# Attention, expert and gated feed-forward in one kernel: the rare-case branch moved to the end, one subtraction moved later in its step, the window limits loaded in one transfer, and other filler matmuls

## The chip, the cores and the metric

The kernel runs on one core of a Trainium2 chip. The metric is the device time of one execution in microseconds; the time before is 661.46 us, the median of three runs (661.29 to 661.57). TensorE's clock has two levels, 1.2 and 2.4 GHz; profiles give it as a granted share, 0.50 or 1.00.

## The reference

Three layers follow each other, in float32.

```python
# 1. attention: 2 batches x 8 heads, 768 positions, head size 64
keep = is_sink | in_window          # the first n_sink=4 keys, or the last window=128
scores = np.where(keep, scale * q @ k.T, -1e9)
x = softmax(scores) @ v             # -> 1536 tokens x 512
# 2. one expert out of 8 per token (argmax of cosine logits), w1 512x1024, w2 1024x512
out[mask] = gate_w[mask, None] * (np.maximum(x[mask] @ w1[e], 0.0) @ w2[e])
# 3. gated feed-forward, 512 -> 1536 -> 512
return ((x @ w_a) * (x @ w_b)) @ w_out
```

n_sink and window are inputs (64-bit integers). The weights of layer 3 arrive as 64-bit floats.

## The kernel before, in words

All products that carry weights run as three matmuls on split operands (high x high, high x low, low x high), so each operand is rounded to a high part and the rest is kept as a low part. After `tc.manual_schedule()` each engine executes its instructions in the order in which the Python code issues them, so this order is the schedule.

**Start.** SP issues the first loads: halves of the first q and k tiles, and between them two broadcasts of n_sink and window (8 bytes to each of 128 partitions each, L193 and L194) into `ctli`. VectorE turns these into float limits and masks (`early_masks`, L222 to L229); the first softmax step (L474) needs the mask. Meanwhile `warm_pe` (L964) issues filler transposes of the identity on TensorE: 8, 4 and 3 of them ahead of the first scores (`WARM`), then 6, 3, 4 and 1 in the first four attention steps (`WARMG`).

**Attention.** 12 blocks of 128 queries with 4 steps each; a step computes two heads' scores (L465; L459 in block 0), softmax, transposes (L490), and the product with v (L521). The block's normalisation and routing (L539 and others) follow some steps later.

**Experts.** Tokens are sorted into slots by expert; the number of slots per expert is planned for common cases. A list `seq` sets the order of matmul groups, and a generator `side_gen` computes the tables for the last layer between them: where each token's row lies in DRAM (`cidx`, and `cide` clipped for the first four tiles), where the output row goes (`ctok`), the squared gate (`gsq`) and a flag `cnt`, which is above zero if limits or expert loads are outside the plan.

**Branch.** After the experts every engine loads `cnt` (L1473) and meets `tc.If(ns_v > 0)` (L1475). Its body recomputes what the plan did not cover and stores rows again; it is not entered with these inputs, so every engine jumps over it.

**Feed-forward.** Three groups of 512 tokens, and for each 12 slices f of 128 hidden units: `ab_mms(f)` makes the two 128x512 products a and b (24 matmuls, L1600 to L1602), `g_split` multiplies them and splits the result, `out_mms` adds the slice to four output tiles (12 matmuls, L1620 to L1622) one slice later. TensorE's order is ab(0), ab(1), out(0), ab(2), out(1) and so on. In the first group `conv_step` also converts the weights of slice f+2 from 64-bit floats, in two half steps per slice; each is a rounding to the high part on ScalarE (`wh`, L1399), two bit operations for the next half (`conv_b0`, L1384 and L1385), the low part (`wl`, L1401) and two further bit operations (`conv_b1`, L1390 and L1391) on VectorE. `g_split` of slice f stands between the two half steps:

```python
nc.scalar.copy(asb, ab[0])
nc.vector.tensor_tensor(out=asb, in0=ab[1], in1=asb, op=ALU.mult)    # L1609
nc.scalar.copy(gh, asb)                                             # L1612
EL[el].tensor_tensor(out=gl, in0=asb, in1=gh, op=ALU.subtract)      # L1613, VectorE
```

The output rows leave by GpSimd's indirect DMAs (L1667).

Of the kernel before, what the change touches and what calls it, by code (L numbers as in the profile page):

```python
# [10 lines left out]
F32 = mybir.dt.float32  # L11
# [51 lines left out]
WARM = [8, 4, 3]  # L63
WARMG = [6, 3, 4, 1]
# [38 lines left out]
TINY = 2.0 ** -15 * 1.125  # L103

# [19 lines left out]
def tile_kernel(ctx, tc, q, k, v, n_sink, window, emb, tau, w1, w2, wc, out, dbg=None):  # L124
# [62 lines left out]
    tt = pc.tile([E, 1], F32, name="tt")  # L187
    q0, k0 = new_q(0, 0), new_k(0, 0)
    for a in (0, W2):
        ld(q0, q, 0, 0, a, a + W2)  # L190
        ld(k0, k, 0, 0, a, a + W2)
        if a == 0:
            nc.sync.dma_start(ctli[:, 0:2], n_sink.bitcast(I32).partition_broadcast(P))  # L193
            nc.sync.dma_start(ctli[:, 2:4], window.bitcast(I32).partition_broadcast(P))  # L194
# [767 lines left out]
    def warm_pe(n):  # L962
        for _ in range(n):
            nc.tensor.transpose(wps, ident, ident)  # L964
# [206 lines left out]
    fe = pool(ctx, "fe", side="right")  # L1171

    def side_gen(w_, pl, psp, tag):
# [172 lines left out]
        V.tensor_copy(cide, cpos[:, 0:4])  # L1346
        G.tensor_scalar(g, g, 1.0 / GSC, None, op0=ALU.mult)
# [16 lines left out]
    wres = {}  # L1364

    raw2, sq2 = {}, {}
# [3 lines left out]
    def load_conv(m):  # L1370
        if m >= NH:
            return
        r = raw2[m] = fe.tile([P, HW, 2], I32, tag="raw", name="raw2", bufs=3)
        nc.sync.dma_start(r.rearrange("p n c -> p (n c)"), wc32[m])

    def conv_abs(m):
        if m < NH:
            sq2[m] = fe.tile([P, HW], F32, tag="sq", name="sq", bufs=2)
            nc.scalar.activation(sq2[m], raw2[m][:, :, 1].bitcast(F32), AF.Abs)  # L1379

    def conv_b0(m):
        if m < NH:
            b, t = sq2[m], sq2[m].bitcast(I32)
            nc.vector.tensor_scalar(b, b, TINY, None, op0=ALU.max)  # L1384
            nc.vector.tensor_scalar(t, t, 5, 2, op0=ALU.logical_shift_left, op1=ALU.logical_shift_right)  # L1385

    def conv_b1(m):
        if m < NH:
            r, t = raw2.pop(m), sq2[m].bitcast(I32)
            nc.vector.scalar_tensor_tensor(t, r[:, :, 0], 29, t, op0=ALU.logical_shift_right, op1=ALU.bitwise_or)  # L1390
            nc.vector.scalar_tensor_tensor(t, r[:, :, 1], -1073741824, t, op0=ALU.bitwise_and, op1=ALU.bitwise_or)  # L1391

    def conv_step(m, wpool):
        f, h = divmod(m, 2)
        if h == 0:
            wres[f] = (wpool.tile([P, CW], F32R, name=f"wh{f}"), wpool.tile([P, CW], F32R, name=f"wl{f}"))
        wh, wl = (t[:, h * HW:(h + 1) * HW] for t in wres[f])
        sq = sq2.pop(m)
        nc.scalar.copy(wh, sq)  # L1399
        conv_b0(m + 1)  # L1400
        nc.vector.tensor_tensor(out=wl, in0=sq, in1=wh, op=ALU.subtract)  # L1401
        conv_abs(m + 2)
        conv_b1(m + 1)
        load_conv(m + 4)

    xh2 = fe.tile([P, NP, TG], F32R, name="xh2")
    xl2 = fe.tile([P, NP, TG], F32R, name="xl2")
    ygs = {}

    def gather_y(u, w=None, rows=None):  # L1410
        ygs[u] = w.tile([P, DM], F32, tag="ygn", name="ygn", bufs=4) if w else fe.tile([P, DM], F32, tag="yg", name="yg", bufs=3)
        early = u < 4 and w is None
        nc.gpsimd.indirect_dma_start(out=ygs[u], out_offset=None, in_=y_d[0:rows or (YR0 if early else YR1), :],  # L1413
                                     in_offset=bass.IndirectOffsetOnAxis(ap=(cide if early else cidx)[:, u:u + 1], axis=0))

    def y_t(u, psp, tag):
        yp = psp.tile([P, NP, P], F32, tag=tag, name="yp2")
        for kc in range(NP):
            nc.tensor.transpose(yp[:, kc, :], ygs[u][:, kc * P:(kc + 1) * P], ident)  # L1419
        return yp  # L1420

    def y_s(u, yp):
        tt = u % 4
        ts_ = slice(tt * P, (tt + 1) * P)
        nc.scalar.copy(xh2[:, :, ts_], yp)
        nc.vector.tensor_tensor(out=xl2[:, :, ts_], in0=yp, in1=xh2[:, :, ts_], op=ALU.subtract)
# [46 lines left out]
    ns_v = nc.values_load(cnt[0:1, 0:1], min_val=0, max_val=4 * int(GENF))  # L1473
    mst.close()
    with tc.If(ns_v > 0):  # L1475
# [97 lines left out]
        with ExitStack() as gs:  # L1573
            xw = pool(gs, "xw3")
            xps = pool(gs, "xps3", space=PSUM)
            for u in range(NU):
                gather_y(u, xw, NBLK * P)
                nc.sync.dma_start(y2_d[u * P:(u + 1) * P, :], ygs[u])
            for u in range(NU):
                yc = xw.tile([P, DM], F32, tag="ygn", name="yc", bufs=4)  # L1580
                nc.sync.dma_start(yc, y2_d[u * P:(u + 1) * P, :])
                nc.sync.dma_start(y_d[u * P:(u + 1) * P, :], yc)
            nc.vector.tensor_copy(cidx, tok)
            for u in range(4):
                gather_y(u, xw, YR1)
                y_s(u, y_t(u, xps, "a"))

    f1 = pool(ctx, "f1")
    f2 = pool(ctx, "f2", bufs=2, side="right")
    fpa = pool(ctx, "fpa", bufs=2, space=PSUM)  # L1590
    fpo = pool(ctx, "fpo", space=PSUM)

    def ab_mms(f):
        wh, wl = wres[f]
        ab = []
        for n in range(2):
            pp = fpa.tile([P, TG], F32, tag="ab"[n], name="pp")
            for kc in range(NP):
                ws = slice(n * 512 + kc * P, n * 512 + (kc + 1) * P)
                nc.tensor.matmul(pp, lhsT=wh[:, ws], rhs=xh2[:, kc, :], start=(kc == 0), stop=False)  # L1600
                nc.tensor.matmul(pp, lhsT=wh[:, ws], rhs=xl2[:, kc, :], start=False, stop=False)  # L1601
                nc.tensor.matmul(pp, lhsT=wl[:, ws], rhs=xh2[:, kc, :], start=False, stop=(kc == NP - 1))  # L1602
            ab.append(pp)
        return ab

    def g_split(f, ab, el):
        asb = f2.tile([P, TG], F32, tag="asb", name="asb", bufs=1)
        nc.scalar.copy(asb, ab[0])  # L1608
        nc.vector.tensor_tensor(out=asb, in0=ab[1], in1=asb, op=ALU.mult)  # L1609
        gh = f2.tile([P, TG], F32R, tag="gh", name="gh", bufs=2)  # L1610
        gl = f2.tile([P, TG], F32R, tag="gl", name="gl", bufs=2)
        nc.scalar.copy(gh, asb)  # L1612
        EL[el].tensor_tensor(out=gl, in0=asb, in1=gh, op=ALU.subtract)  # L1613
        return f, gh, gl

    def out_mms(po, f, gh, gl, done=None, tts=range(4)):
        wh, wl = wres[f]
        for tt in tts:
            ts_ = slice(tt * P, (tt + 1) * P)
            nc.tensor.matmul(po[tt], lhsT=gh[:, ts_], rhs=wh[:, 1024:CW], start=(f == 0), stop=False, skip_group_check=True)  # L1620
            nc.tensor.matmul(po[tt], lhsT=gh[:, ts_], rhs=wl[:, 1024:CW], start=False, stop=False, skip_group_check=True)  # L1621
            nc.tensor.matmul(po[tt], lhsT=gl[:, ts_], rhs=wh[:, 1024:CW], start=False, stop=(f == NF - 1), skip_group_check=True)  # L1622
            if done is not None:
                done(tt)

    NG = NT // TG
    outs = []
    pend = None
    tail = []
    for gi in range(NG):  # L1630
        po = [fpo.tile([P, DM], F32, tag=f"po{tt}", name=f"po{tt}") for tt in range(4)]
        for f in range(NF):
            ab = ab_mms(f)
            more = gi == 0 and f + NF0 < NF
            if more:
                conv_step(2 * (f + NF0), f1)
            cur = g_split(f, ab, 'V')
            if more:
                conv_step(2 * (f + NF0) + 1, f1)
            u0 = 4 * (gi + 1)  # L1640
            if f == NF - 2 and gi + 1 < NG:
                for tt in range(3):
                    gather_y(u0 + tt)
            if f == NF - 1 and gi + 1 < NG:
                yps = [y_t(u0 + tt, fpa, "ab"[tt]) for tt in range(2)]
                gather_y(u0 + 3)
                for tt in range(2):
                    y_s(u0 + tt, yps[tt])
            if pend is not None:
                if gi == NG - 1 and f == NF - 1:  # L1650
                    out_mms(*pend, tts=range(3))
                    tail.append(pend)
                else:
                    out_mms(*pend)
            pend = (po, *cur)
        if gi + 1 < NG:
            yps = [y_t(u0 + tt, fpa, "ab"[tt - 2]) for tt in range(2, 4)]
# [67 lines left out]
```

## Time and profile before

| | |
|---|---|
| median of three runs | 661.46 us (661.29 to 661.57) |
| profiled execution, its own time | 659.85 us |
| its span, first to last instruction | 658.0 us |
| busy: TensorE / VectorE / ScalarE / GpSimd | 628.6 / 396.4 / 304.8 / 122.2 us |
| granted TensorE clock, mean | 0.977 |

The span is what the profile's rows are placed in; the own time has 1.85 us more around it. Rows give a start, a duration, an engine, a line of the kernel, an operation with its tiles (out<-in), and in brackets the idle time before it with what ended it. TensorE stands as PE (matmuls) and PEld (weight loads), VectorE as DVE, ScalarE as ACT, GpSimd as POOL, SyncE as SP; a q behind an engine's name is its sequencer, which waits, branches and issues.

### The profile page before, as it was taken

The numbers are of one execution on the slowest core, as the hardware profiler recorded it, in microseconds if no ns is written. First come the engines' busy times: TensorE is split into PE (matmuls) and PEld (weight loads), VectorE is DVE, ScalarE is ACT, GpSimd is POOL, SyncE is SP. The second block draws the span as 40 slices with busy tenths as digits, with TensorE's granted clock in tenths as the row PEclk, the third lists the DMA queues.
The fourth block names the chain that finished last, engine by engine and source line by source line (L and its number), as shares of the span: only waits on it lengthen the run. The fifth ranks groups of instructions, "written<-read, shape, count | busy, mean of one in ns | idle before, by whom it ended". The sixth has DMA issues, their size and how long they took to land. (4 is left out here: it accounts for less than half of the span.)

```text
span 658.0 us, 10420 instructions
## 1 busy us (share of the span) xinstructions
PE 628.6 (96%) x3665; PEld 515.4 (78%) x3665; DVE 396.4 (60%) x910; ACT 304.8 (46%) x581; POOL 122.2 (19%) x269
## 2 busy tenths in 40 slices
PE   8999999889999999998969999999999999999995
PEld 5777777779998989887858767678888888888884
DVE  5688878998888766798839999943111113111111
ACT  4678777667575657667524444422111113111111
POOL 7243345481042211020010000004000003000002
PEclk7699999989999999999979999999999999999999
DMA  4244325323787887587253454203000002000001
GB/s 144 85 160 130 130 81 191 147 76 134 254 289 273 269 280 267 180 304 253 86 177 134 154 186 150 96 17 114 0 1 0 1 0 81 0 1 1 0 1 64
DMA packets 25967, 80.77 MB, mean 123 GB/s; under 512 B 3560, under 2 KB 4072, under 8 KB 25904
## 3 DMA queue, kind: packets, MB, share of 16 engines
q1 hardware_dynamic: 22560, 69.23, 31.5%
q0 software_dynamic: 3344, 10.77, 4.8%
q8 instruction: 31, 0.51, 0.3%
q14 instruction: 32, 0.26, 0.1%
HBM read 81.82 MB, written 10.75 MB: 141 GB/s over the span
## 5 line engine op out<-in xcount | busy, mean ns | idle before, releaser
L1600 PE MATMUL pp<-xh,wh 128*128 128x512 f32 x288 | 114.5, 398 | 5.7 <-DVEq L1475 5.7
L1609 DVE TENSOR_TENSOR asb<-pp,asb 128x512 f32<-128x512 f32 x36 | 24.8, 689 | 151.5 <-PE pp L1602 151.5
L1601 PE MATMUL pp<-xl,wh 128*128 128x512 f32 x288 | 114.9, 399 | 0.0
L1602 PE MATMUL pp<-xh,wl 128*128 128x512 f32 x288 | 114.6, 398 | 0.0
L603 DVE TENSOR_TENSOR lo<-raw,hi 128x1024 fp32r<-128x1024 f32 x80 | 96.1, 1228 | 7.9 <-ACT hi L595 6.2
L595 ACT CAST hi<-raw 128x1024 fp32r<-128x1024 f32 x87 | 88.0, 1050 | 7.8 <-PE hp L708 4.1
L1600 PEld LDWEIGHTS pp<-xh,wh 128*128 128x128 f32 x288 | 54.7, 190 | 19.4 <-ACTq L1475 6.2
L1601 PEld LDWEIGHTS pp<-xl,wh 128*128 128x128 f32 x288 | 54.8, 190 | 13.1
L1602 PEld LDWEIGHTS pp<-xh,wl 128*128 128x128 f32 x288 | 54.8, 190 | 12.9
L1612 ACT CAST gh<-asb 128x512 fp32r<-128x512 f32 x36 | 22.3, 620 | 90.2 <-DVE asb L1609 87.4
L1608 ACT COPY asb<-pp 128x512 f32<-128x512 f32 x36 | 21.0, 583 | 89.6 <-PE pp L1602 89.5
L1620 PE MATMUL po<-wh,gh 128*128 128x512 f32 x144 | 57.9, 402 | 3.9 <-ACT gh L1612 3.9
L477 ACT ACTIVATE p<-st,mn 128x260 f32<-128x260 f32 (+1 forms) x96 | 46.6, 487 | 29.2 <-DVE mn L474 22.8
L1622 PE MATMUL po<-wh,gl 128*128 128x512 f32 x144 | 57.6, 400 | 0.0
L1621 PE MATMUL po<-wl,gh 128*128 128x512 f32 x144 | 56.8, 394 | 0.0
L1413 POOL DMA_INDIRECT yg<-y_d,cidx x8 | 8.3, 1040 | 215.6 <-PE yp L1419 187.3
L780 PE MATMUL hT<-pxh,hi 128*128 128x256 f32 x160 | 45.5, 285 | 0.0
L782 PE MATMUL hT<-pxh,lo 128*128 128x256 f32 x160 | 44.7, 280 | 0.0
L781 PE MATMUL hT<-pxl,hi 128*128 128x256 f32 x160 | 44.7, 279 | 0.0
L474 DVE CUSTOM_DVE_ANT_0 st<-sc,m 128x260 f32<-128x260 f32 (+1 forms) x96 | 35.0, 399 | 10.4 <-PE sc L465 5.1
L1379 ACT ACTIVATE sq<-raw 128x768 f32<-128x768 f32 x24 | 22.1, 923 | 39.4 <-DVE wl L1401 39.4
L1613 DVE TENSOR_TENSOR gl<-asb,gh 128x512 fp32r<-128x512 f32 x36 | 24.9, 692 | 24.8 <-ACT gh L1612 24.8
(344 smaller groups left out, 1335.1 us busy)
## 6 DMA issues: line engine op xcount, KB each, us to landing
raw<-in_moe_w_dram SPq DMA_DIRECT2D x88, 512.0 KB
raw<-in_moe_w_dram SPq DMA_DIRECT2D x24, 768.0 KB
y_d<-ys SPq DMA_DIRECT2D x16, 256.0 KB
vt<-in_v_dram SPq DMA_DIRECT2D x12, 256.0 KB
x_d<-xl SPq DMA_DIRECT2D x12, 256.0 KB
qt<-in_q_dram SPq DMA_DIRECT2D x11, 256.0 KB
kt<-in_k_dram SPq DMA_DIRECT2D x10, 256.0 KB
qt<-in_q_dram SPq DMA_DIRECT2D x2, 128.0 KB
```

The source lines that it names most:

```text
L477: nc.scalar.activation(p[:, j, 0:W], st[:, 0:W], AF.Exp, bias=z['mn'][:, h:h + 1], scale=-1.0, accum_out=z['sm'][:, h:h + 1])
L595: ER = {'A': lambda o, i: nc.scalar.copy(o, i), 'V': lambda o, i: nc.vector.tensor_copy(o, i), 'P': lambda o, i: nc.gpsimd.tensor_copy(o, i)}
L603: EL[elo].tensor_tensor(out=lo, in0=raws[g], in1=hi, op=ALU.subtract)
L780: nc.tensor.matmul(hT[:, c, :], lhsT=hi[:, ws], rhs=z['xh'][:, kc, :], start=(c == 0 and kc == 0), stop=False, skip_group_check=True)
L781: nc.tensor.matmul(hT[:, c, :], lhsT=hi[:, ws], rhs=z['xl'][:, kc, :], start=False, stop=False, skip_group_check=True)
L782: nc.tensor.matmul(hT[:, c, :], lhsT=lo[:, ws], rhs=z['xh'][:, kc, :], start=False, stop=(kc == NP - 1), skip_group_check=True)
L1600: nc.tensor.matmul(pp, lhsT=wh[:, ws], rhs=xh2[:, kc, :], start=(kc == 0), stop=False)
L1601: nc.tensor.matmul(pp, lhsT=wh[:, ws], rhs=xl2[:, kc, :], start=False, stop=False)
L1602: nc.tensor.matmul(pp, lhsT=wl[:, ws], rhs=xh2[:, kc, :], start=False, stop=(kc == NP - 1))
L1620: nc.tensor.matmul(po[tt], lhsT=gh[:, ts_], rhs=wh[:, 1024:CW], start=(f == 0), stop=False, skip_group_check=True)
L1621: nc.tensor.matmul(po[tt], lhsT=gh[:, ts_], rhs=wl[:, 1024:CW], start=False, stop=False, skip_group_check=True)
L1622: nc.tensor.matmul(po[tt], lhsT=gl[:, ts_], rhs=wh[:, 1024:CW], start=False, stop=(f == NF - 1), skip_group_check=True)
```

## The change

- The two broadcasts of n_sink and window become one, of an array `limits` that holds both, issued from ScalarE's queue ahead of all other loads.
- The fillers become fp32 matmuls of the identity with itself. Ahead of the first scores there are 6, 2 and 2; in the first six attention steps 4, 3, 4, 1, 2 and 2.
- The functions of the feed-forward are wrapped so that they can be issued twice (`ffn_parts`, `ffn_run`). The first issue stands straight behind the experts, with no branch ahead of it; the flag is loaded on every engine in its third group, at slice 2, with a hint that the branch will be taken. The branch stands behind the whole feed-forward; its body repeats the feed-forward after the recomputation.
- As row numbers in `cidx` are no longer checked by the branch ahead of the gathers, `side_gen` makes a copy `cidc` clipped to the stored rows, with two further small VectorE instructions and one further step of the generator.
- `g_split` returns the subtraction that makes `gl` as a function. Where a half step of the weight conversion follows, this function is called inside it, behind `conv_b0` and ahead of `wl`.

```diff
-WARM = [8, 4, 3]
-WARMG = [6, 3, 4, 1]
+WARM = [6, 2, 2]
+WARMG = [4, 3, 4, 1, 2, 2]
...
+    nc.scalar.dma_start(ctli, lim.bitcast(I32).partition_broadcast(P))
     q0, k0 = new_q(0, 0), new_k(0, 0)
     for a in (0, W2):
         ld(q0, q, 0, 0, a, a + W2)
         ld(k0, k, 0, 0, a, a + W2)
-        if a == 0:
-            nc.sync.dma_start(ctli[:, 0:2], n_sink.bitcast(I32).partition_broadcast(P))
-            nc.sync.dma_start(ctli[:, 2:4], window.bitcast(I32).partition_broadcast(P))
...
-            nc.tensor.transpose(wps, ident, ident)
+            nc.tensor.matmul(wps, lhsT=ident, rhs=ident, start=True, stop=True)
...
+        yield
+        V.tensor_scalar(cpos[:, 4:NU], cpos[:, 4:NU], 0.0, float(YR1 - 1), op0=ALU.max, op1=ALU.min)
+        V.tensor_copy(cidc, cpos)
...
-    def conv_step(m, wpool):
+        def conv_step(m, wpool, mid=None):
...
             nc.scalar.copy(wh, sq)
             conv_b0(m + 1)
+            if mid:
+                mid()
             nc.vector.tensor_tensor(out=wl, in0=sq, in1=wh, op=ALU.subtract)
             conv_abs(m + 2)
             conv_b1(m + 1)
             load_conv(m + 4)
...
-    ns_v = nc.values_load(cnt[0:1, 0:1], min_val=0, max_val=4 * int(GENF))
     mst.close()
-    with tc.If(ns_v > 0):
...
+    def ffn_run(z, stack, tag):
...
             nc.scalar.copy(gh, asb)
-            EL[el].tensor_tensor(out=gl, in0=asb, in1=gh, op=ALU.subtract)
-            return f, gh, gl
+            return f, gh, gl, lambda: EL[el].tensor_tensor(out=gl, in0=asb, in1=gh, op=ALU.subtract)
...
                 ab = ab_mms(f)
+                if not slow and (gi, f) == (NG - 1, 2):
+                    ns.append(nc.values_load(cnt[0:1, 0:1], min_val=0, max_val=4 * int(GENF)))
+                    tc.mark_branch_hint_location("cover", "LikelyTaken")
                 more = gi == 0 and f + NF0 < NF
                 if more:
                     conv_step(2 * (f + NF0), f1)
-                cur = g_split(f, ab, 'V')
+                *cur, low = g_split(f, ab, 'V')
                 if more:
-                    conv_step(2 * (f + NF0) + 1, f1)
+                    conv_step(2 * (f + NF0) + 1, f1, low)
+                else:
+                    low()
...
+    ns = []
+    ffn_run(ff, fz, "")
+    fz.close()
+    ns_v = ns[0]
+
+    with tc.If(ns_v > 0, label="cover"):
...
+            ffn_run(ffn_parts(pool(gs, "fes", side="right"), True), gs, "s")
```

## Rows read from the trace of the kernel before

**Rows 1.** Windows: length, busy (count) per engine, granted clock, DMA share, GB/s.

```profile
24.00:26.00 2.00, 2.00 (x13) 1.66 (x10) 0.65 (x4) 1.10 (x4) 0.00 (x0) 0.50 0.06 22
28.00:30.00 2.00, 2.00 (x22) 1.70 (x22) 1.61 (x8) 1.10 (x4) 0.79 (x3) 1.00 0.00 0
335.00:337.00 2.00, 2.00 (x5) 1.59 (x6) 0.00 (x0) 0.83 (x1) 0.40 (x1) 0.50 0.07 19
450.00:520.00 70.00, 70.00 (x303) 56.61 (x302) 12.45 (x18) 11.31 (x19) 4.87 (x6) 1.00 0.07 22
```

**Rows 2.** Timeline of PE around the branch: start us, us, engine, line, operation.

```profile
328.66 0.40 PE L802 MATMUL yp<-lo,hh 128*128 128x512 f32 x1
334.80 0.77 PE L1600 MATMUL pp<-xh,wh 128*128 128x512 f32 x1 [5.74 <-DVEq L1475]
```

**Rows 3.** The branch's line on its sequencers: durations in ns, first and last start.

```profile
L1475 POOLq EVENT_SEMAPHORE  x6: 17/30/43, 311.4 to 314.5; - x6
L1475 DVEq EVENT_SEMAPHORE  x2: 21/21/21, 334.6 to 334.7; - x2
L1475 POOLq COMPARE_BRANCH  x1: 58/58/58, 308.8 to 308.8; - x1
L1475 POOLq INC_SWDGE_SEM  x1: 660/660/660, 314.6 to 314.6; - x1
L1475 DVEq COMPARE_BRANCH  x1: 72/72/72, 328.4 to 328.4; - x1
```

**Rows 4.** Timeline of DVE, from the branch to the first slice's product.

```profile
327.64 1.28 DVE L1426 TENSOR_TENSOR xl<-yp,xh 128x512 fp32r<-128x512 f32 x2
343.44 0.69 DVE L1609 TENSOR_TENSOR asb<-pp,asb 128x512 f32<-128x512 f32 x1 [1.94 <-PE pp L1602]
```

**Rows 5.** Timeline of DVE, ACT and PE in a slice of group one; slice 9.

```profile
410.48 0.68 DVE L1609 TENSOR_TENSOR asb<-pp,asb 128x512 f32<-128x512 f32 x1
411.84 0.69 DVE L1613 TENSOR_TENSOR gl<-asb,gh 128x512 fp32r<-128x512 f32 x1 [0.68 <-ACT gh L1612]
412.45 0.55 DVE L1384 TENSOR_SCALAR sq<-sq 128x768 f32<-128x768 f32 x1
413.52 0.95 DVE L1401 TENSOR_TENSOR wl<-sq,wh 128x768 fp32r<-128x768 f32 x1
...
411.72 0.83 ACT L1399 CAST wh<-sq 128x768 fp32r<-128x768 f32 x1
...
429.61 0.68 DVE L1609 TENSOR_TENSOR asb<-pp,asb 128x512 f32<-128x512 f32 x1
...
431.72 0.50 PE L1622 MATMUL po<-wh,gl 128*128 128x512 f32 x1
```

**Rows 6.** Timeline of all engines at the start.

```profile
1.53 3.46 PE L964 MATMUL wps<-ident 128*128 128x128 f32 x15 [1.53 <-POOL ident masks.py:199]
...
2.10 0.43 SPq L194 DMA_DIRECT2D ctli<-in_window_dram  x1
...
5.90 0.21 DVE L222 CAST ctl<-ctli 128x4 f32<-128x4 int32 x1 [5.04 <-DMA ctli<-in_window_dram]
...
7.90 0.29 DVE L474 CUSTOM_DVE_ANT_0 st<-sc,m 128x128 f32<-128x128 f32 x1 [0.15 <-DVE m L229]
```

**Rows 7.** Timeline of PE: first scores of blocks one to three, four fp32 matmuls.

```profile
14.67 0.59 PE L465 MATMUL sc<-kh,qh 64*128 64x260 f32 x2
...
24.70 1.33 PE L539 MATMUL bk<-R,oT 128*128 128x144 f32 x4
...
26.82 0.39 PE L465 MATMUL sc<-kh,qh 64*128 64x260 f32 x2
...
35.74 0.39 PE L465 MATMUL sc<-kh,qh 64*128 64x260 f32 x2
```

**Rows 8.** Timeline of POOL: the last output DMA.

```profile
652.62 0.97 POOL L1667 DMA_INDIRECT out_dram<-os__11394,ctok  x1 [0.22 <-ACT os__11394 L1663]
```

**Rows 9.** The kernel's closing line on GpSimd's sequencer: durations in ns, starts.

```profile
L1721 POOLq DRAIN  x3: 46/115/4799, 652.4 to 657.8; - x3
```

More of the change, by code (lines that the diff above doesn't have):

```diff
@@ L1 @@
 import math
+from types import SimpleNamespace
 from contextlib import ExitStack
@@ L103 @@
 TINY = 2.0 ** -15 * 1.125
+FFN = ('load_conv', 'conv_abs', 'conv_b0', 'conv_b1', 'conv_step', 'gather_y', 'y_t', 'y_s')
 def rsqrt(nc, pool, ss, shape, tag):
@@ L123, in tile_kernel @@
 @with_exitstack
-def tile_kernel(ctx, tc, q, k, v, n_sink, window, emb, tau, w1, w2, wc, out, dbg=None):
+def tile_kernel(ctx, tc, q, k, v, lim, emb, tau, w1, w2, wc, out, dbg=None):
     nc = tc.nc
@@ L1170, in tile_kernel @@
     cide = rt.tile([P, 4], I32, name="cide")
-    fe = pool(ctx, "fe", side="right")
+    cidc = rt.tile([P, NU], I32, name="cidc")
+    fz = ctx.enter_context(ExitStack())
+    fe = pool(fz, "fe", side="right")
     def side_gen(w_, pl, psp, tag):
@@ L1363, in tile_kernel @@
     wc32 = wc.bitcast(I32)
-    wres = {}
-    raw2, sq2 = {}, {}
     HW = CW // 2
     NH = 2 * NF
[L1370 to L1391, printed above, removed]
@@ L1393, in conv_step @@
-    def conv_step(m, wpool):
[L1394 to L1414, printed above, removed]
@@ L1428, in tile_kernel @@
+    ff = ffn_parts(fe, False)
+    load_conv, conv_abs, conv_b0, conv_b1, conv_step, gather_y, y_t, y_s = (getattr(ff, x) for x in FFN)
     side = side_gen(rw1, pl, xps, "xp")
@@ L1573, in tile_kernel @@
         with ExitStack() as gs:
[L1574 to L1612, printed above, removed]
-        EL[el].tensor_tensor(out=gl, in0=asb, in1=gh, op=ALU.subtract)
-        return f, gh, gl
[L1616 to L1636, printed above, removed]
-            cur = g_split(f, ab, 'V')
-            if more:
-                conv_step(2 * (f + NF0) + 1, f1)
[L1640 to L1657, printed above, removed]
-        def done(tt, gi=gi, po=po):
-            os_ = fe.tile([P, DM], F32, tag="yg", name="os_", bufs=3)
-            u = gi * 4 + tt
-            if tt % 2:
-                nc.scalar.activation(os_, po[tt], AF.Copy, scale=gsq[:, u:u + 1])
-            else:
-                nc.vector.tensor_scalar(os_, po[tt], gsq[:, u:u + 1], None, op0=ALU.mult)
-            nc.gpsimd.memset(warm, 0.0)
-            ins = nc.gpsimd.indirect_dma_start(out=out, out_offset=bass.IndirectOffsetOnAxis(ap=ctok[:, u:u + 1], axis=0), in_=os_, in_offset=None)
-            for o in outs:
-                tc.declare_no_dep(ins.ins, o.ins, reason="the rows of out that two tiles write are disjoint")
-            outs.append(ins)
-        if gi + 1 < NG:
-            for tt in range(2):
-                y_s(u0 + 2 + tt, yps[tt])
-        if gi + 1 < NG:
-            out_mms(*pend, done)
-        else:
-            out_mms(*pend, done, (0, 1, 2))
-            out_mms(*tail[0], tts=(3,))
-            out_mms(*pend, done, (3,))
-        pend = None
@@ L1683 @@
-_INS = ['q', 'k', 'v', 'n_sink', 'window', 'moe_expert_emb', 'moe_tau', 'moe_w1', 'moe_w2', 'moe2_w']
+            ffn_run(ffn_parts(pool(gs, "fes", side="right"), True), gs, "s")
+_INS = ['q', 'k', 'v', 'limits', 'moe_expert_emb', 'moe_tau', 'moe_w1', 'moe_w2', 'moe2_w']
 def _laid_out(np, a):
@@ L1693, in _laid_out @@
     return dict(
+        limits=np.concatenate([np.asarray(a['n_sink']).reshape(1), np.asarray(a['window']).reshape(1)]),
         q=heads_first(np.asarray(a['q'])),
```

159 lines of the change are left out of this document (149 added, 10 removed).

## The prediction

> **What bounds the kernel now.** I read the windows first, then each engine's timeline where TensorE stops. From 450 to 520 us TensorE is busy in 70.00 of 70 us and issues 303 matmuls, 0.231 us each [rows 1]; a slice of the feed-forward has 36 of them, so at least 8.3 us. In groups two and three nothing but TensorE counts. The first group is different. The product `asb` of slice 0 starts at 343.44 and that of slice 9 at 429.61 [rows 4, 5]: nine steps of 9.574 us, 1.2 us above what TensorE needs. There VectorE sets the pace: it carries two half steps of weight conversion, `asb` and `gl`, and it pauses once in each slice, 0.68 us ahead of `gl`, for ScalarE's `gh` [rows 5]. Ahead of this group stands the branch: TensorE issues its last expert matmul at 328.66 and its next at 334.80, released by VectorE's sequencer [rows 2]; at 335 to 337 its granted clock is 0.50 [rows 1], after this pause. At the start, VectorE waits 5.04 us for the window limit [rows 6].
>
> **The branch ahead of the feed-forward.** VectorE's branch is at 328.4 and its first event behind it at 334.6 [rows 3]: 6.2 us. With straight code, `ab` of slice 0 can start when VectorE has written the last low parts: 327.64 + 1.28 = 328.92 [rows 4]. Its 24 matmuls at 0.231 are 5.6 us; with 0.3 for the last one's end and the wait, `asb` of slice 0 starts at 334.8 in place of 343.44, **8.6 us earlier**. Of this, 5.9 is the pause (334.80 against 328.92), the rest is the slower clock, which without a pause has no cause to fall. Next late would be VectorE: before this `asb` it has one half step, 3.8 us (half of a slice's 9.574 without the pause of 0.75 worked out below and two operations of 0.61), and ends it about 333, and ScalarE's `wh` is ahead of that. So TensorE is the last. If memory that the experts' tiles held comes free late, some of it is lost; I count that in the range.
>
> **asb and gl apart.** On VectorE `asb` starts at 410.48 and `gl` at 411.84. `gl` itself takes 0.61 from its start to that of the next instruction (412.45), and `asb`, of the same size, the same; so the pause is 1.36 - 0.61 = 0.75 us from issue to issue [rows 5]. Behind the change `conv_b0` stands there, 413.52 - 412.45 = 1.07 us of work that needs no `gh`; it covers the 0.75 whole. `gl` then starts 1.68 after `asb`, while `gh` is there at 1.36. `wl` follows at 2.29; its `wh` ends on ScalarE at 411.72 + 0.83 = 412.55, 2.07 after `asb`: still covered, by 0.2 us. A step falls from 9.574 to 8.82 us. Nine steps give 9 x 0.75 = **6.8 us**. In the last of them no next half is left to convert, so `gl` waits there as before. What does `gl` hold up? It is 0.3 us later after `asb`, and TensorE's third matmul of `out` waits for it. TensorE however would be at work: 372 matmuls lie ahead of `out` of slice 9, at 0.231 they end at 328.92 + 85.9 = 414.9, and `gl` of slice 9 is there at 334.8 + 9 x 8.82 + 2.05 = 416.2, where that third matmul stood at 431.72 [rows 5]. So VectorE remains the bound of this group, by about a microsecond, and the two edits together bring 8.6 + 6.8 = 15.4 us. They can't bring over 16.8 (414.9 against 431.72). If `gl` brings nothing, 8.6 remain, or 7 with late memory.
>
> **Limits in one transfer.** The window's broadcast is issued at 2.10 and the cast that waits for it starts at 5.90; the first softmax step follows 2.0 us later, with VectorE at work on the masks between [rows 6]. One broadcast at the head of ScalarE's queue can be issued about 1.4 us earlier, and the first of two broadcasts is gone from in front of it, half of the 256 small packets. I take 1.9 us; below, nothing at all (if q and k's halves are then late), above 2.5. What is late next is the scores: 10 fillers in place of 15, 3.46 us for 15 [rows 6], end 1.2 us earlier, so the scores are there. The loads of q and k lose two issues ahead of them on SP. Gain **1.9 us**.
>
> **Fillers.** A filler transpose costs 0.23 us (3.46 for 15) [rows 6]; four fp32 matmuls of 144 columns took 1.33 us [rows 7] at a granted clock of 0.50 [rows 1], so 0.33 each, 0.30 for 128 columns. Those ahead of the scores are hidden behind the limits. Four further ones, in steps 4 and 5, fall between 14.67 and 26.82, where TensorE is busy throughout at the lower clock, as at 24 to 26 [rows 1, 7]; they cost 4 x 0.21, some **0.85 us** (0 if something else is late, 1.2 at 0.30). The transposes' row is the nearest, as it has the same operands and 128 columns of fp32; I take 0.21, an estimate of its 0.23 without the first one's latency.
>
> **The branch at the end, the flag and the small tables.** The flag's load on every engine stands in group three, where TensorE has work queued without a gap and the others are mostly idle [rows 1]: nothing; without that cover about one restart of TensorE, 0.50 us as for the matmul behind a wait [rows 5]. Two small VectorE instructions among the experts: nothing, under 0.2 each. The branch itself comes behind each engine's last work. GpSimd issues the last output transfer at 652.62 and its drain, started at 652.4, lasts 4.8 us, to 657.2 [rows 8, 9]; under this most engines can jump. GpSimd can't: at the old place it needed 2.6 us from branch to first event (308.8 to 311.4) and a further 0.66 for its transfer count [rows 3]. Half of the former is hidden by the landing. I take **+1.0 us**; below 0, above 5.4 (653.6 + 6.2 as on VectorE, and 0.66 + 1.8 + 0.8 for count, drain and end, against 658.0).
>
> **The sum.** 15.4 + 1.9 - 0.85 - 1.0 = 15.45 us. From the profiled execution's own 659.85 this leaves 644.4. The median of the runs is 1.6 above that, so I forecast **646.0**.
>
> **The rivals.**
> A. *Clock up early.* Block one (first scores 14.67 to 26.82) took 12.15 us with clock 0.50 inside, block two 8.92 (to 35.74) with 1.00 [rows 1, 7]. If the clock of block one is up, 3.2 us go, and the four fillers cost 0.4 less: 642.4. For it: TensorE gets more work in steps 4 and 5. Against it: TensorE was busy in all of 24 to 26, with four full fp32 matmuls and others among the transposes, and was still at 0.50 [rows 1, 7]. The Trainium skill (TensorE: Matmul & The Clock Gate, Part 4: PE-mode transpose) says that transposes don't count as busy for the clock as matmuls do. By that rule the fillers now lift the clock and this rival's time is the forecast; the trace has only transposes as fillers and can't show it.
> B. *Apart doesn't pay.* If VectorE still waits (for `wh`, with 0.2 us to spare), the step stays 9.57: 646.0 + 6.8 = 652.8. Rows 5 speak against it.
> C. *The branch comes back at the end.* At 5.4 in place of 1.0 us: 650.4. The Trainium skill (Runtime: NRT & Kernel Launch, Instruction fetch mechanics) says that a taken branch to a page that isn't at hand stalls for its fetch; rows 3 agree (2.6 to 6.2 us). Against it: the hint, and the closing drain as cover.
> D. *Slower.* The clock doesn't rise after block one, as fewer fillers stand ahead of the scores. Each further block at 0.50 costs 12.15 - 8.92 = 3.23 us; from five blocks on the gain of 15.45 is gone, ten blocks give 678. Against it: in block one, with few fillers, the clock rose.
>
> **How the numbers follow.** Forecast 0.54, A 0.22, B 0.10, C 0.10, D 0.04. The forecast's own range is 644.2 to 648 (limits 0 to 2.5, end 0 to 3). For 8 in 10 it must hold A and most of C: 641.5 to 650.6; B and D and the edges are left out. Faster by over 0.2% (1.3 us, about what a measurement of this kernel can tell): all but D and a sliver, 0.95; same 0.01; slower 0.04.
>
> **What would show it.** Right: TensorE without a pause between the experts and the feed-forward; `asb` starts 8.8 us apart in the first group; `gl` without a wait; the first softmax step near 6.0. Wrong: an `asb` spacing of 9.5; more than 2 us between GpSimd's last transfer and the end than now; a granted clock of 1.00 in block one (A) or 0.50 in block three (D).

## The result and the profile after

The changed kernel takes 642.69 us (median of 4 runs, 642.09 to 643.21) against 661.38 (660.43 to 661.57) of the kernel before, timed beside it: a ratio of 0.972, 95% interval 0.9703 to 0.9737. The time lies in the range, 3.3 us below the forecast, and at the number of rival A. The profiled execution took 642.09, with a span of 640.2 us; before it was 659.85 and 658.0, so 17.8 us of span have gone.

The map of the span shows first where the clock differs. This is the line of the granted clock on the page, in 40 slices of some 16 us, before:

```profile
PEclk7699999989999999999979999999999999999999
```

and after:

```profile
PEclk9999999999999999999999999999999999999997
```

Before, it sinks in the first two slices, in the ninth (143 to 146 us) and in the 21st (behind the branch). After, none of these is left. (The first digits flatter on both lines, as experiment one shows.) The 7 at the end is in the last 16 us, which hold the end of TensorE's work.

The start of the kernel after, on the timeline (start us, us, engine, line, operation, and in brackets the idle time before it with its releaser):

```profile
1.53 4.64 PE L964 MATMUL wps<-ident 128*128 128x128 f32 x20 [1.53 <-POOL ident masks.py:199]
...
3.83 0.51 DVE L222 CAST ctl<-ctli 128x4 f32<-128x4 int32 x1 [2.97 <-DMA ctli<-in_limits_dram]
...
5.37 0.35 DVE L226 SCALAR_TENSOR_TENSOR m<-rel,lims,ge 128x128 f32<-128x128 f32 x1
...
6.09 0.76 PE L459 MATMUL sc<-kf,qt 64*128 64x128 f32 x4
...
6.89 0.29 DVE L474 CUSTOM_DVE_ANT_0 st<-sc,m 128x128 f32<-128x128 f32 x1 [0.52 <-PE sc L459]
...
12.97 0.50 PE L465 MATMUL sc<-kh,qh 64*128 64x260 f32 x2 [0.37 <-DVE mn L474]
...
22.02 0.39 PE L465 MATMUL sc<-kh,qh 64*128 64x260 f32 x2
...
30.94 0.39 PE L465 MATMUL sc<-kh,qh 64*128 64x260 f32 x2
```

Beside [rows 6, 7]: the limits are there 2.07 us earlier (cast at 3.83 in place of 5.90), but the first softmax step is only 1.01 earlier (6.89): it now waits 0.52 us for the scores, and VectorE takes longer from the cast to the window mask (L226), 1.54 us in place of 0.85. The ten fillers are 20 matmul rows of 0.23 us. Block one takes 9.05 us (12.97 to 22.02) in place of 12.15, as block two does (8.92).

Between the experts and the feed-forward, and in a slice of group one (slice 5, followed by the `asb` of slice 9):

```profile
322.27 0.39 PE L802 MATMUL yp<-lo,hh 128*128 128x512 f32 x1
323.34 0.50 PE L1513 MATMUL pp<-xh,wh 128*128 128x512 f32 x1 [0.68 <-ACT ys L595]
...
329.18 0.69 DVE L1522 TENSOR_TENSOR asb<-pp,asb 128x512 f32<-128x512 f32 x1 [2.31 <-PE pp L1515]
...
373.17 0.68 DVE L1522 TENSOR_TENSOR asb<-pp,asb 128x512 f32<-128x512 f32 x1
...
374.83 0.68 DVE L1526 TENSOR_TENSOR gl<-asb,gh 128x512 fp32r<-128x512 f32 x1
375.44 0.95 DVE L1409 TENSOR_TENSOR wl<-sq,wh 128x768 fp32r<-128x768 f32 x1
...
408.31 0.68 DVE L1522 TENSOR_TENSOR asb<-pp,asb 128x512 f32<-128x512 f32 x1
```

Where TensorE stood for 5.74 us [rows 2], it now stands for 0.68, by the profile waiting for ScalarE's read of an expert's output. `gl` and `wl` have no bracket: VectorE doesn't wait ahead of them. Nine steps take 79.13 us, 8.79 each, against 9.574 [rows 5].

The end, where the last `asb`, the last tile of the output and its transfer stand:

```profile
623.45 0.69 DVE L1522 TENSOR_TENSOR asb<-pp,asb 128x512 f32<-128x512 f32 x1 [6.33 <-PE pp L1515]
...
630.66 0.69 ACT L1580 ACTIVATE os__7002<-po,gsq 128x512 f32<-128x512 f32 x1 [3.09 <-DVEq L1605]
...
631.62 0.96 POOL L1584 DMA_INDIRECT out_dram<-os__7002,ctok  x1 [0.77 <-ACT os__7002 L1580]
```

the new branch's line on the sequencers (durations in ns, first and last start):

```profile
L1605 POOLq EVENT_SEMAPHORE  x6: 17/30/43, 634.2 to 634.6; - x6
...
L1605 POOLq COMPARE_BRANCH  x1: 58/58/58, 631.4 to 631.4; - x1
...
L1605 DVEq COMPARE_BRANCH  x1: 72/72/72, 627.6 to 627.6; - x1
...
L1605 POOLq INC_SWDGE_SEM  x1: 1060/1060/1060, 634.7 to 634.7; - x1
```

and the closing line:

```profile
L1745 POOLq DRAIN  x3: 46/109/3586, 635.8 to 640.0; - x3
```

From the last transfer's start to the end of the span it is now 8.6 us (640.2 - 631.62), where it was 5.4 (658.0 - 652.62) [rows 8]. The last `asb` of before, for the sum:

```profile
645.00 0.69 DVE L1609 TENSOR_TENSOR asb<-pp,asb 128x512 f32<-128x512 f32 x1 [6.33 <-PE pp L1602]
```

These landmarks cut the span into pieces, and the pieces add up to the whole difference:

| piece | before | after | difference | forecast |
|---|---|---|---|---|
| to the last expert matmul (limits, fillers) | 328.66 | 322.27 | -6.39 | -1.9 + 0.85 |
| from there to `asb` of slice 0 (branch) | 14.78 | 6.91 | -7.87 | -8.6 |
| nine steps of group one (apart) | 86.17 | 79.13 | -7.04 | -6.8 |
| `asb` of slice 9 to the last `asb` | 215.39 | 215.14 | -0.25 | 0 |
| last `asb` to last transfer | 7.62 | 8.17 | +0.55 | in the next |
| last transfer to the end | 5.38 | 8.58 | +3.20 | +1.0 for both |
| sum | 658.0 | 640.2 | -17.8 | -15.45 |

The two terms of the feed-forward hold to within a microsecond. The first row is 5.3 us better than forecast and the end 2.75 worse. The experiments go to these two, and check the other two.

### The profile page after: what moved, and what is told of

It is laid out like the page before. It is cut to its first block, busy times and chain, and to the rows that moved or that the text cites. A ratio compares the mean times of both kernels' runs of the same rounds, so it can differ in the third digit from the quotient of the medians.

```text
span 640.2 us, 10451 instructions
## 1 busy us (share of the span) xinstructions
PE 616.5 (96%) x3688; PEld 510.7 (80%) x3688; DVE 395.6 (62%) x912; ACT 304.4 (48%) x581; POOL 118.2 (18%) x269
## 4 chain that ended last, share of the span: by engine, by line
PE 70%; issue 17%; DVE 6%; ACT 3%; POOL 2%; DMA 1%; POOLq 0%; DVEq 0%; ACTq 0%
PE pp L1513 7%; PE pp L1514 7%; PE pp L1515 7%; PE hp L708 5%; PE po L1534 3%; PE po L1533 3%; PE po L1532 3%; PE ou L521 3%; PE hT L782 3%; PE hT L780 3%; PE hT L781 3%; PE yp L800 3%; PE yp L802 3%; PE yp L801 3%; PE sc L465 2%
## 5 line engine op out<-in xcount | busy, mean ns | idle before, releaser
L1514 PE MATMUL pp<-xl,wh 128*128 128x512 f32 x288 | 113.6, 394 | 0.0
L1421 POOL DMA_INDIRECT yg<-y_d,cidc x8 | 8.1, 1014 | 200.4 <-PE yp L1426 172.2
```

## The experiments

Times are medians; a ratio is to the kernel before, run beside it on the same chip, with its 95% interval. That kernel's own median on the three chips was 659.74 (experiments one, two, six and seven), 660.98 (three, five, eight and nine) and 660.1 (four and ten). The changed kernel itself ran only beside experiments four and ten, so other differences to it are between chips; it gave 642.69 in the result and 642.63 there. Unless an experiment says otherwise, its edit is made in the changed kernel.

**One: the old kind of filler, same numbers.** Does the kind of instruction lift the clock?

```diff
-            nc.tensor.matmul(wps, lhsT=ident, rhs=ident, start=True, stop=True)
+            nc.tensor.transpose(wps, ident, ident)
```

> The changed kernel with its fillers as transposes again, in the same numbers (6, 2, 2 and 4, 3, 4, 1, 2, 2). Theory K (kind: transposes do not count for the clock, matmuls do) and theory B (busy time: a filler matmul occupies TensorE for two rows of 0.23 us, a transpose for one, so these fillers are half as long) both expect the granted clock at 0.50 again in most of block one, so block one's first scores to block two's take about 12 us in place of 9.05. The first softmax step comes earlier than 6.89, near 6.4, as the scores no longer wait for 4.6 us of fillers. Time 645.0 to 646.5. A third theory (neither: the earlier limits alone moved the attention against the clock) expects the clock at 1.00 and 642.2.

643.61 us (643.13 to 645.86), ratio 0.976 (0.9723 to 0.9797). Both theories expected 645.0 to 646.5 and about 12 us for block one; only the profiled run, of 645.86, lies there, and its block one took 10.74 us. Its timeline of TensorE, first scores of blocks one and two:

```profile
13.46 0.58 PE L465 MATMUL sc<-kh,qh 64*128 64x260 f32 x2
...
24.20 0.39 PE L465 MATMUL sc<-kh,qh 64*128 64x260 f32 x2
```

and one window of the same kernel (length, busy and count of PE, PEld, DVE, ACT, POOL, granted clock, DMA share, GB/s):

```profile
13.00:20.00 7.00, 7.00 (x39) 4.83 (x37) 4.74 (x22) 4.25 (x15) 2.09 (x7) 1.00 0.74 232
```

The window reads 1.00 although the pair of matmuls took 0.58 us, as at 0.50 before (0.59 in block one, 0.39 in blocks two and three [rows 7]). The trace holds changes of the clock alone, and in this one the first is a rise, at 20.81 us; what stands ahead of it is shown as 1.00. So at the start of a kernel the matmuls' durations are read, not the window. With this, block one of this kernel was at the lower of the two levels, 1.2 GHz, up to 20.81, and at 2.4 GHz behind it.

**Two: the old kind, twice the number.** An fp32 matmul of the identity leaves two rows of 0.23 us and a transpose one. With twice the transposes the time on TensorE is nearly the same, and only the kind differs from the changed kernel.

```diff
-WARM = [6, 2, 2]
-WARMG = [4, 3, 4, 1, 2, 2]
+WARM = [12, 4, 4]
+WARMG = [8, 6, 8, 2, 4, 4]
...
+            nc.tensor.transpose(wps, ident, ident)
```

> The changed kernel with transposes in twice the numbers (12, 4, 4 and 8, 6, 8, 2, 4, 4): as much TensorE time in fillers as with the matmuls. Theory K (kind) expects the clock as with single transposes: 0.50 in block one, which takes about 12 us, time 645.5 to 646.5. Theory B (busy time) expects the clock at 1.00 from about 6.7 us on, block one at 9.05 us and 642.7 as with the matmuls.

642.96 us (642.09 to 643.41), ratio 0.9753 (0.9714 to 0.9791): the changed kernel's time. On the timeline the 20 transposes take 4.53 us, the 20 matmul rows 4.64, and block one lasts 8.99 us (13.21 to 22.20), with the scores' pair at 0.50 and 0.39:

```profile
1.53 4.53 PE L964 MATMUL wps<-ident 128*128 128x128 f32 x20 [1.53 <-POOL ident masks.py:199]
...
13.21 0.50 PE L465 MATMUL sc<-kh,qh 64*128 64x260 f32 x2 [0.41 <-DVE mn L474]
...
22.20 0.39 PE L465 MATMUL sc<-kh,qh 64*128 64x260 f32 x2
```

The trace records the rise at 7.56 us; in the changed kernel it is at 6.68. So it isn't the kind: transposes that keep TensorE at work as long did the same.

**Three: the new fillers alone, in the kernel before.** All else is as before; `WARM`, `WARMG` and the matmul in `warm_pe` are the new ones.

> The kernel before with nothing changed but the fillers: fp32 matmuls in the new numbers. Theory: the clock is up from about 7 us on, block one takes about 9.05 us in place of 12.15, the experts lose a stretch at the lower clock; together 4 us, time 657. As the first softmax step is still bound by the limits (7.90), the fillers ahead of the scores cost nothing here. Rival: the earlier limits were needed for the clock (the work meets it otherwise late): block one stays at 11 to 12 us, time 660 to 661.

655.97 us (654.32 to 656.36) against 660.98, ratio 0.9924 (0.9898 to 0.995): 5.0 us for the fillers alone. The timeline of the profiled run, the fastest of five:

```profile
7.90 0.29 DVE L474 CUSTOM_DVE_ANT_0 st<-sc,m 128x128 f32<-128x128 f32 x1 [0.15 <-DVE m L229]
...
13.79 0.35 PE L465 MATMUL sc<-kh,qh 64*128 64x260 f32 x1 [0.42 <-DVE mn L474]
...
22.90 0.39 PE L465 MATMUL sc<-kh,qh 64*128 64x260 f32 x2
```

The first softmax step stands where it stood [rows 6], block one takes 9.11 us, and the last expert matmul is at 323.27, 5.39 earlier than before [rows 2]. The changed kernel has it at 322.27: what the limits, with the other small edits ahead of that point, bring beside the fillers is 1.0 us.

**Four: the old fillers in the changed kernel** (`WARM` 8, 4, 3 and `WARMG` 6, 3, 4, 1, transposes), run beside the changed kernel and the kernel of experiment one once more.

> The changed kernel with the fillers of before (transposes, 8, 4, 3 and 6, 3, 4, 1). Theory B (the clock follows TensorE's busy time, and the new fillers are what adds it): the clock is at 0.50 in most of block one as before, block one about 11 to 12 us, time 645.5 to 647. Rival: the earlier limits alone have moved the attention so that the clock rises early: block one near 9, time 643.

> The changed kernel itself, beside the others on this chip: 642.1 to 643.2 as before, granted share 0.991 to 0.995, in a narrower spread than with transposes, if more TensorE time in fillers makes the early rise of the clock certain.

> The changed kernel with transposes in the new numbers, once more, beside the changed kernel itself on one chip. The first time its profiled run took 645.86 with the clock up at 20.81, while its other runs took 643.1 to 643.7. If the moment at which the clock rises differs from run to run, the runs spread over 643 to 646 with granted shares of 0.987 to 0.993 again, longer by about 0.5 us for each 0.001 less. If it was one odd run, all are near 643.4 now.

Old fillers: 646.86 us (646.37 to 647.27), ratio 0.9808 (0.9783 to 0.9833). Changed kernel: 642.63 (641.62 to 643.56), ratio 0.9745 (0.9719 to 0.9771). The new fillers bring 4.2 us here. With the old ones block one takes 11.82 us, and the window inside shows the lower level (this is behind the first recorded change):

```profile
16.00:25.00 9.00, 9.00 (x50) 6.52 (x50) 5.06 (x23) 5.54 (x17) 0.00 (x0) 0.50 0.26 84
```

Fifty matmul rows in 9 us, all of it busy; the changed kernel has 74 in its 9, with 0.69 us to spare:

```profile
13.00:22.00 9.00, 8.31 (x74) 6.17 (x74) 7.57 (x37) 7.18 (x25) 2.09 (x7) 1.00 0.65 229
```

With the old fillers the clock does rise early, but it falls again. The trace of this run records a rise at 5.29 us, a fall at 15.53 and the next rise at 25.77; that of the kernel before a rise at 6.34, a fall at 9.76 and a rise at 26.82. Here are windows of the kernel before:

```profile
6.00:8.00 2.00, 0.84 (x6) 0.60 (x4) 1.58 (x8) 0.00 (x0) 1.67 (x12) 1.00 1.05 365
8.00:10.00 2.00, 1.70 (x11) 1.35 (x12) 1.90 (x14) 1.21 (x6) 1.38 (x4) 0.94 0.62 228
10.00:12.00 2.00, 2.00 (x10) 1.50 (x9) 1.97 (x11) 2.00 (x10) 0.20 (x1) 0.50 0.00 0
```

The durations say the same: a pair of transposes of the attention (L490) takes 0.38 us at 9.27 and 0.64 at 11.53. Ahead of the fall TensorE had stood for 1.41 us, waiting for the first softmax step; with the old fillers in the changed kernel it was busy for only 0.27 us of the microsecond from 12 to 13. In the changed kernel it is busy throughout from 2 to 12 us, and the clock stays up:

```profile
6.00:8.00 2.00, 2.00 (x15) 1.61 (x16) 1.45 (x8) 0.78 (x4) 1.76 (x11) 1.00 0.83 306
```

The kernel of experiment one gave 641.39, 643.05, 643.69, 645.09, 645.53 and 645.62: a spread of 4.2 us where the changed kernel's is 1.9. Its profiled run, of 645.62, again has the rise late, at 20.66. Its best run is as fast as the best of the changed kernel (641.62). With that number of transposes some runs are as fast as with matmuls and most are not; that the moment of the rise makes the difference is shown for the profiled runs alone. The runs' granted shares, which were expected to follow the time, don't: 0.991 at 645.62, 0.986 at 643.69.

**Five: fewer fillers ahead of the scores.** Three, one and one there, and nine in place of four in the first attention step, so that the scores aren't late.

```diff
-WARM = [6, 2, 2]
-WARMG = [4, 3, 4, 1, 2, 2]
+WARM = [3, 1, 1]
+WARMG = [9, 3, 4, 1, 2, 2]
```

> The changed kernel with half of its first ten fillers moved behind the first scores (3, 1, 1 and 9, 3, 4, 1, 2, 2). Theory: the first scores start near 4.1 in place of 6.09 and the first softmax step at 6.4, bound by the mask, in place of 6.89; the clock rises as before the move, since TensorE is as busy; time 642.2. Rival: the nine fillers behind the first scores delay the second step's scores by 1.5 us or the clock rises later; time 643 to 645.

643.36 us (642.07 to 645.34), ratio 0.9745 (0.9708 to 0.9783). No gain: two of the four runs took 642.1 and 642.2, the other two 644.5 and 645.3. In the profiled run, the fastest, the clock's rise is at 5.70. The scores start at 4.18 and the first softmax step at 6.53, without a wait for them:

```profile
4.18 0.80 PE L459 MATMUL sc<-kf,qt 64*128 64x128 f32 x4
...
6.53 0.29 DVE L474 CUSTOM_DVE_ANT_0 st<-sc,m 128x128 f32<-128x128 f32 x1 [0.15 <-DVE m L229]
```

but block one starts at 12.84, 0.13 earlier than in the changed kernel: of the 0.36 us at the first step a third is left there, less than the runs can tell apart.

**Six: `gl` straight behind `asb` again.**

```diff
                 *cur, low = g_split(f, ab, 'V')
+                low()
                 if more:
-                    conv_step(2 * (f + NF0) + 1, f1, low)
-                else:
-                    low()
+                    conv_step(2 * (f + NF0) + 1, f1)
```

> The changed kernel with gl issued straight behind gh again, as before. Theory: VectorE's step in group one goes back from 8.79 to 9.57 us, nine steps are 7.0 us, time 649.7. Rival: TensorE was the bound of group one and the spacing came from elsewhere (memory freed late, the branch): the step stays below 9.0 and the time below 645.

649.93 us (648.79 to 650.86), ratio 0.986 (0.982 to 0.99): 7.2 us slower than the changed kernel. A step is 9.602 us, and the wait is back:

```profile
377.34 0.68 DVE L1522 TENSOR_TENSOR asb<-pp,asb 128x512 f32<-128x512 f32 x1
378.71 0.69 DVE L1526 TENSOR_TENSOR gl<-asb,gh 128x512 fp32r<-128x512 f32 x1 [0.68 <-ACT gh L1525]
```

Nine steps of 0.81 more make 7.3 us, as much as the two profiles differ (647.5 and 640.2): the order is the whole effect, and rival B is out.

**Seven: no branch at the end.** The branch, its hint and its body (the recomputation and the second feed-forward) go; the flag is loaded but not tested.

```diff
-                    tc.mark_branch_hint_location("cover", "LikelyTaken")
...
-    with tc.If(ns_v > 0, label="cover"):
-        ...
```

> The changed kernel without the branch at the end and its body (left out: the recovery for inputs outside the plan; the flag is still loaded). Theory: the span grew by 3.2 us between GpSimd's last transfer and the end (5.38 before, 8.57 behind the change) because GpSimd's drain starts only behind its jump, six events and the transfer count. It then falls to 5.4 us and the time to 639.5. Rival: the drain is late for another reason (the landing of the last rows): the distance stays at 8 us or more and the time at 642.7. In between, as far as the drain's own 3.59 us is a fixed cost: 641.

638.53 us (638.16 to 639.43), ratio 0.9688 (0.9651 to 0.9726), 4.2 below the changed kernel. The last transfer follows the last `asb` by 7.60 us and the end follows the transfer by 5.46 (636.7 - 631.24), both as before the change:

```profile
631.24 0.97 POOL L1583 DMA_INDIRECT out_dram<-os__7002,ctok  x1 [0.19 <-issue]
```

From the last `asb` to the end it is 13.1 us here and 16.75 in the changed kernel: the branch at the end costs 3.7 us in the profile and 4.2 in the medians.

**Eight and nine: the hint.** Without the hint, and with it moved from slice 2 of the last group to its last slice.

> The changed kernel without the hint for the branch at the end. Theory: the hint hides nothing; behind the change GpSimd still needed 2.8 us from its branch (631.39) to its first event (634.18), as 2.6 at the old place. Then this distance stays at 2.6 to 3.0 and the time at 642.7. Rival: the hint saves part of the fetch; the distance grows by 1 us or more and the time to 643.7 or above.

> The changed kernel with the hint moved from the third slice of the last group to its last slice, 80 us nearer to the branch. Theory: if a hint works but its page is lost again over 80 us, GpSimd's distance from branch to first event falls from 2.8 us to under 1 and the time by 1.5 to 2 us, to 641. Rival: the hint does nothing at this branch; 2.8 us and 642.7 as they are.

642.31 us (641.63 to 643.44), ratio 0.9725 (0.9693 to 0.9757), and 642.18 (642.11 to 643.45), ratio 0.9724 (0.9692 to 0.9756): both are the changed kernel's time. GpSimd's jump without the hint:

```profile
L1604 POOLq EVENT_SEMAPHORE  x6: 17/30/43, 633.7 to 634.1; - x6
...
L1604 POOLq COMPARE_BRANCH  x1: 58/58/58, 630.9 to 630.9; - x1
```

and with it late:

```profile
L1606 POOLq EVENT_SEMAPHORE  x6: 17/30/43, 634.3 to 634.7; - x6
...
L1606 POOLq COMPARE_BRANCH  x1: 58/58/58, 631.6 to 631.6; - x1
```

2.8, 2.7, and 2.8 in the changed kernel: the hint does nothing at either place.

**Ten: the two waits that the straight code left.** The banks that the `po` tiles take and those of `pp` are exchanged, so that the first `pp` isn't behind ScalarE's read of an expert's output; the last output tile gets the memory of `asb` in place of the third buffer of `yg`.

```diff
-        fpa = pool(stack, "fpa" + tag, bufs=2, space=PSUM)
         fpo = pool(stack, "fpo" + tag, space=PSUM)
+        fpa = pool(stack, "fpa" + tag, bufs=2, space=PSUM)
...
-                os_ = fe.tile([P, DM], F32, tag="yg", name="os_", bufs=3)
+                if gi == NG - 1 and tt == 3:
+                    os_ = f2.tile([P, DM], F32, tag="asb", name="os_", bufs=1)
+                else:
+                    os_ = fe.tile([P, DM], F32, tag="yg", name="os_", bufs=3)
```

> A version meant to beat the changed kernel: the output tiles' PSUM pool opened ahead of the products' pool, so that the first product does not take the bank that the last expert rows are copied from (0.68 us of waiting at 323.34), and the last output tile put in the free asb buffer, so that ScalarE need not wait for a row buffer until the first output transfer has landed (630.58). Theory: the first asb starts 0.7 us earlier, GpSimd's last transfer 0.6 us earlier against the last asb; time 641.4 to 641.8. Rival: both were hidden (VectorE is the bound of group one, GpSimd's transfers follow each other 1.27 us apart anyway): 642.7.

641.48 us (640.43 to 642.33), ratio 0.9724 (0.9698 to 0.9751), beside 642.63 of the changed kernel: 1.15 less. Over six runs each the means are 641.36 and 642.60, apart by 1.2 with an interval of about 0.2 to 2.3 worked out from the scatter of the runs (0.84 and 0.78). So it is the fastest here of those that keep the branch, by little. The places show it:

```profile
322.52 0.39 PE L802 MATMUL yp<-lo,hh 128*128 128x512 f32 x1
322.75 0.40 PE L1513 MATMUL pp<-xh,wh 128*128 128x512 f32 x1
...
628.14 0.69 ACT L1583 ACTIVATE os__7002<-po,gsq 128x512 f32<-128x512 f32 x1 [1.41 <-PE po L1534]
...
630.20 0.97 POOL L1587 DMA_INDIRECT out_dram<-os__7002,ctok  x1 [0.19 <-issue]
```

TensorE goes from the experts to the feed-forward without a pause: from the last expert matmul to the first `asb` it is 5.99 us (328.51 - 322.52) in place of 6.91. Counted from the last `asb` (here at 622.61), the last tile is begun 1.7 us sooner (5.53 in place of 7.21), but GpSimd issues its four transfers 1.28 us apart, so the last one comes only 0.58 sooner (7.59), and 0.3 of that is lost behind it (8.9 us to the end in place of 8.6).

## Why the prediction was right or wrong, point by point

**The branch ahead of the feed-forward: right, 7.87 of 8.6.** The missing 0.7 is the pause of 0.68 that the prediction had kept for "memory that the experts' tiles held"; experiment ten takes it away and gets 0.92. The lower clock behind the branch [rows 1] went with the pause, as argued. This term is read from the rows; no run puts the branch alone back.

**asb and gl apart: right, 7.04 against 6.8**, shown by taking it back (7.2). That VectorE remains the bound of group one is right too: a step of 8.79 is still above the 8.3 that TensorE needs.

**Limits: the transfer right, its worth half.** It came 2.07 us earlier (forecast 1.9), and 1.01 was left at the first softmax step. Two steps of the prediction failed. "The first softmax step follows 2.0 us later": even where it doesn't wait for the scores, in experiment five, it follows 2.66 us after the cast (3.87 to 6.53). Four small VectorE instructions (L222 to L225) take 1.54 us, from 3.83 to 5.37 in the changed kernel, where they took 0.85 before, from 5.90 to this row:

```profile
6.75 0.35 DVE L226 SCALAR_TENSOR_TENSOR m<-rel,lims,ge 128x128 f32<-128x128 f32 x1
```

That is 0.69 us; why they are slower there is open. "The scores are there" cost the other 0.36 (6.89 against 6.53 in experiment five): the prediction had the fillers end 1.2 us earlier than before, taking ten fillers at 0.23, and they ended 1.2 later, at 0.46 each. Moving half of them behind the scores, as experiment five does, doesn't gain it back.

**Fillers: the step that failed.** The prediction priced them (+0.85) and left the clock alone. They brought 5.4 us in the span with nothing else changed; in the medians it is 5.0 there and 4.2 in the changed kernel. 0.9 of it is there when block one starts (13.79 against 14.67), 3.0 is block one (9.11 against 12.15 us). The other 1.5 come later: the stretch near 143 us, where the clock before is at 0.50 though TensorE is busy throughout, has gone:

```profile
143.00:146.00 3.00, 3.00 (x16) 3.00 (x16) 2.80 (x4) 1.05 (x2) 2.73 (x2) 0.50 0.47 169
```

after, at the same place in the work:

```profile
140.00:144.00 4.00, 4.00 (x36) 4.00 (x35) 4.00 (x6) 3.67 (x5) 3.70 (x4) 1.00 0.45 76
```

The matmul that starts this stretch, at 142.02 before, is 3.91 us earlier in experiment three, the one that ends it, at 146.20, is 5.40 earlier, and the last expert matmul 5.39. Ahead of both stretches TensorE pauses for the same 2.2 us (from 139.85 before, from 135.07 after). The drop is in all four profiles with the old fillers or with transposes in the new numbers (before, experiment one and its repeat, the old fillers of experiment four), and in none of the ten others. Why it is spared there, 130 us behind the fillers, is open; nothing run here separates it.

The price itself was misread too. The "four fp32 matmuls of 144 columns" [rows 7] are two: L539 issues 48 matmuls in the whole kernel and leaves 96 rows. In the end no cost shows: block one, with four further fillers, takes 9.05 us and block two, without any, 8.92.

**Rival A came about, for a reason that the rule behind it doesn't give.** By the Trainium skill (TensorE: Matmul & The Clock Gate, Part 4: PE-mode transpose) the new kind would be the cause. Experiment two has transposes alone and the clock rises nearly as early (7.56 us) and the time is the same: here the measurement decides against the kind. The kernel before speaks against it as well: its fillers are transposes, with one pair of fp32 scores behind the first 15, and its clock rose at 6.34. What differs between experiment one and the changed kernel, the kind apart, is the time that the fillers keep TensorE at work: 2.40 us ahead of the scores for ten transposes, 4.64 for ten matmuls. It needn't all stand ahead of the scores: in the profiled run of experiment five it is 2.50 ahead of them and 2.64 right behind. The argument that the prediction held against A, that a TensorE busy from 24 to 26 stayed at 0.50 [rows 1, 7], wasn't wrong as a reading, but it was read too late: in the kernel before the clock was up from 6.34 and lost at 9.76, ahead of block one. So the new fillers do two things that the runs show apart: against half as much filler work (experiment one) the clock rises earlier, and against the old fillers (before, experiment four) it doesn't fall again. Which of the fillers keep it up isn't separated.

**The end: right in kind, +3.75 against +1.0, nearer to rival C's 5.4.** The prediction let half of GpSimd's jump hide under the landing of the last transfer. That overlap is the step that failed: the drain starts behind jump, events and count. The rows show it as a chain: branch 631.4, events 634.2 to 634.6, count 634.7 for 1.06 us, drain 635.8 for 3.59. The landing isn't what the end waits for: the last transfer landed 2.7 us after its issue, ahead of the drain, and the drain is still as long as the time from the end of the last transfer's instruction to the end of the drain before (3.6 us: 652.62 + 0.97 to 657.2 [rows 8, 9]) and in experiment seven (3.6 us, to 635.8). So the whole stretch of some 3.2 us between that instruction and the drain is added. The sum was loose as well: half of 2.6 and 0.66 make 2.0 and not 1.0, and the terms of the bound of 5.4 add up to 5.1, with 1.8 us for a drain that no row shows at that length.

The other 0.55 is ahead of the last tile, which waits for a row buffer. Before and in experiment seven ScalarE waits there 2.52 and 2.48 us for the landing of the first output transfer; after the change it is 3.09, put down to VectorE's sequencer at its branch, though that transfer, too, landed only 3.3 us after its issue. Which of the two it was isn't separated. Without the branch (experiment seven) it is 7.60 us from the last `asb` to the last transfer, and with memory of its own for the tile (experiment ten) 7.59. The hint, held against C, is no cover.

**The forecast's value.** Fillers 6.25 better (-5.4 for +0.85), end 2.75 worse, limits 0.9 worse, the branch ahead 0.75 worse, the slices 0.5 better: 2.35 us in the sum by the profile (17.8 against 15.45). The medians are 3.3 apart: the profiled run before was 1.6 faster than the median that the prediction started from, the one after 0.6 faster than its own. So it is in part by luck that the time lies in the stated range. The forecast's own 644.2 to 648 was missed; with the fillers' 6.25 alone the time would have been 639.8, below the range, and it was the losses at the end and at the limits that brought it back, to rival A's number. Of the prediction's own signs of being wrong two came: over 2 us more between the last transfer and the end (3.2), and the clock up in block one. Rival D fell in the first profile: no block after the first is at the lower clock.

## What to carry to other kernels

A pause that an in-order engine makes for another engine's cast costs its length in every step as long as that engine is the bound; an operation that needs nothing from there, put between, gave it back whole here. A branch moved from the middle to the end still has to be paid by the engine that ends last: count its jump, its events and its transfer count one after the other, ahead of the closing drain. What counted here for the fillers at the start was the time that they keep TensorE at work, not their kind; look for where the clock falls again as well as for where it rises, and try them over several runs, since one number of them can be fast in one run and slow in the next.

## What the runs showed of the hardware that was not expected

- An fp32 matmul of 128 columns is two rows of 0.23 us each at the start (20 rows for ten), a transpose of the same operands one (15 rows for 15).
- From branch to first event, GpSimd took 2.8 us at the end of the kernel (3.2 in experiment ten), VectorE 3.0 (627.6 to 630.6) and ScalarE 3.2 (630.7 to 633.9); at the old place it was 2.6 for GpSimd and 6.2 for VectorE [rows 3]. A hint some 80 us ahead or in the last slice changes nothing.
- GpSimd's transfer count at the join took 0.66 us in the middle and 1.06 at the end.
- GpSimd's closing drain took 3.6 us behind its last work in the profiles before, after and of experiments seven and ten, whether or not a branch had kept it waiting.
- The granted clock is shown as 1.00 up to the first change that the trace recorded, whatever it was.
